# The start of a weight load and the order of all compute queues in an attention and GLU block on one core

## The chip, the cores and the metric

The kernel runs on one core of one Trainium2 chip. A core has a matrix engine (TensorE, here PE; its weight loads are shown apart as PEld), a vector engine (VectorE, DVE), a scalar engine (ScalarE, ACT), a general engine (GpSimd, POOL) and SyncE (SP), which here only issues DMA transfers. Each engine works through its own queue in order, and engines wait for one another by semaphores. Matrix products land in PSUM, which has eight banks of 2 KB in each of 128 partitions; everything else lies in SBUF.

The metric is the device time of one execution in microseconds (us); lower is better. Results are given as a median over several executions, and one further execution is recorded by the hardware profiler.

## The reference

The reference is a transformer block of two halves on one sequence of S = 2048 tokens with D = 448 channels, in bfloat16. The first half is a linear attention with a learned feature map (16 heads of 28 channels), the second a gated feed-forward part with F = 1792.

```python
B, S, D = x.shape
H = 16; Dh = D // H
n = _layernorm(x)                                   # (x - mean) / sqrt(var + 1e-5)
q, k, v = split((n @ wqkv), heads)                  # each (H, S, Dh)
pq = einsum("bhsd,hdf->bhsf", q, w_phi)
pk = einsum("bhsd,hdf->bhsf", k, w_phi)
phi_q = concatenate([_softmax(pq), _softmax(-pq)], axis=-1)     # 56 features
phi_k = concatenate([_softmax(pk), _softmax(-pk)], axis=-1)
kv = einsum("bhsf,bhsd->bhfd", phi_k, v)            # sums over all 2048 tokens
z  = einsum("bhsf->bhf", phi_k)
num = einsum("bhqf,bhfd->bhqd", phi_q, kv)
den = einsum("bhqf,bhf->bhq", phi_q, z)[..., None] + 1e-6
h = x + (num / den) @ wo
n2 = _layernorm(h)
out = h + (_sigmoid(n2 @ w_gate) * (n2 @ w_up)) @ w_down
```

The sums `kv` and `z` need every token, so no token's `num` can be computed before the last token has been added to them. That is the one full stop in the middle of the block.

## The kernel before, in words

**Tiles.** The sequence is cut into 16 tiles of 128 tokens, numbered 0 to 15; `name_t` or `namet` is the operation `name` on tile `t`. Four tiles make a chunk of 512 tokens, numbered by `c`. The 448 channels are held as four slabs of 128 rows that overlap in part, and most matrix products run as two chains at once, one on rows 0 to 63 and one on rows 64 to 127 of the array. The helper `both` (L328, its matmul on L333) issues them alternately, so nearly all of PE's work stands under line 333 in the profile, and is told apart by its tensors. A product cut in two such steps has the names `...a` and `...b`.

**The graph and its order.** The function `build` describes 1029 operations with what each reads and writes. `Graph` derives the waits from that. The order on each engine is not derived: it is written out by hand in the dictionary `ORDER` (L249 on), one list of names for each of the queues `sp`, `act`, `pe`, `dve` and `pool`. An operation that may run on several engines runs on the one in whose list its name stands. The dictionary `PACE` (L312) adds further dependencies by hand: `{"ld_wg1": "kva14"}` lets the load `ld_wg1` wait until PE has finished `kva14`. Since queues are in order, whatever stands behind a waiting operation waits with it.

**The first stage: keys and values.** For each tile, DVE takes the statistics (`bst` L552, `agg` L553). POOL takes the power -1/2 of the variance (`pow1`, L561) and, where the normalising engine needs it, the negated mean (`nm1`, L560) and their product (`nb1`). `xn` (L580) normalises, on DVE, POOL or ACT, into one of five buffers. Tiles 0 to 3 are transposed on PE (`xT0` to `xT3`) and copied out by `xT0e` to `xT3e` (L538); tiles 4 to 15 are transposed by DMA on SP's queue (`xT`, L590). Meanwhile the feature map is folded into the key and the query weights: `w2m0` (keys, from a PE transpose `wT`) and `w2m1` (queries, from DMA transposes `ld_q0` to `ld_q3`, L507), both L619, with the copies `w2e0` (L628) and `w2e1` (L636). `warm` operations are products of zeros.

Then PE makes a tile's key features in bank 0 or 1 and its values in bank 2 or 3: `ppa ppb vva vvb` for two tiles at once (tiles 0 to 3), `pva pvb` for one (tiles 4 to 15). ACT takes the exponentials of the features and of the negated features (`ek`, two instructions, L678 and L679), DVE or ACT copies the values (`v1`, L538). DVE sums (`ss`, L682) and inverts (`rs`, L688), and POOL or DVE multiplies (`phi`, L692). There are five buffers for `ek` and `v1` and four for `phi`. `kva` and `kvb` add a tile's products into banks 6 and 7 (L333, `psum<-v,phi`). `seed` writes there first.

**Queries and output of the attention.** `pqa` and `pqb` make the query features of a chunk in two banks, `eqc_ip` and `eqc_im` (ACT, L730) their exponentials. After the last `kv` step, `kvzA` to `kvzD` copy the sums with a mask out of banks 6 and 7 (DVE L759 or ACT L763). `qs` sums the exponentials of tiles 0 and 1. For each tile follow `num` on PE, and `rsm qq b c rden` on DVE (L807 to L815), which put the two softmaxes' shares together; `o` divides (L819, POOL or DVE) and `oT` transposes (PE for tiles 0 and 1, else DMA). `wof` or `woa` and `wob` multiply with `wo`; `h` adds the residual (L845), and `nm sq ve pow2 hn hT` (L849 to L868) are the second layer norm and its transpose (DVE or POOL, ACT, DVE or POOL, POOL, DVE or POOL, SP).

**The gated part.** The chunks of it are named by their first tile and cover 2, 2, 4, 4 and 4 tiles: 0, 2, 4, 8 and 12. For each of 14 slices `f` of F, `gac_f` and `gbc_f` make gate and up products in two banks, `sig` (ACT, L919) takes the sigmoid into one of four buffers, and `hh` (L925) multiplies. For the names in `UCOPY` (most of chunk 0 and all of chunk 2) ACT first copies the up product into one of the five `xn` buffers (`uc`, L924), and then `hh` may run on POOL as well as on DVE. `dn dp dm dl` multiply with `w_down`; `fin` (L959) adds the residual and `out` stores.

**Loads.** SP's queue issues the loads in this order: tiles of `x`, the key, value and query weights, the transposes `xT4` to `xT15`, `wo` (784 KB in four transfers), gate and up weights (`ld_wg0 ld_wu0` to `ld_wg3 ld_wu3`, 448 KB each, two of them half of that), `w_down` (224 KB each), then the transposes and stores of the rest. All load instructions stand on L434. PE asks for all eight gate and up loads at once, in the empty operation `wgu`, ahead of `num6` and `ga0_1`.

**What the change touches.** `ORDER` and `PACE`, and through `ORDER` the engine on which 33 operations run. The functions that follow take their order and their engine from these two.

Of the kernel before, what the change touches and what calls it, by code (L numbers as in the profile page):

```python
# [18 lines left out]
class Graph:  # L19
# [109 lines left out]
    def emit(self, nc):  # L129
# [120 lines left out]
    ),  # L250
    "act": (
# [11 lines left out]
    ),  # L263
# [22 lines left out]
    ),  # L286
    "dve": (
# [15 lines left out]
    ),  # L303
    "pool": (
# [5 lines left out]
    ),  # L310
}
PACE = {"ld_wg1": "kva14"}  # L312
UCOPY = "0_2 0_3 0_4 0_5 0_6 0_7 0_8 0_9 0_10 0_11 0_12 0_13 2_0 2_1 2_2 2_3 2_4 2_5 2_6 2_7 2_8 2_9 2_10 2_11 2_12 2_13".split()
PROGRAM = (
# [35 lines left out]
def build(nc, A_x, A_wqkv, A_w_phi, A_wo, B_w_gate, B_w_up, B_w_down, out):  # L350
# [10 lines left out]
    with ExitStack() as es:  # L361
# [630 lines left out]
        at = {o.name: o.i for o in g.ops}  # L992
        for a, b in PACE.items():
            g.ops[at[a]].deps[at[b]] = False
# [36 lines left out]
```

## Time and profile before

| | |
|---|---|
| Median of 3 executions | 205.1 us (204.98 to 205.74) |
| The profiled execution | 205.9 us |
| Its span, first to last instruction | 204.0 us |
| Granted PE clock | 1.00 |
| PE busy | 195.4 us (96%) |
| PE weight loads | 112.7 us (55%) |
| DVE busy | 127.1 us (62%) |
| ACT busy | 99.8 us (49%) |
| POOL busy | 67.1 us (33%) |
| DMA | 16.25 MB, mean 80 GB/s |

Times inside the execution are counted from the start of the span. A row of the groups or of a timeline gives the line of the program, the engine, the instruction and its tensors (result, arrow, inputs), partitions and elements, and how many there are. In a timeline the first number is the start and the second the time; a square bracket at the end says how long the engine had stood idle just before, and which engine and tile ended that. "issue" there means that the engine waited for nothing that the profile shows. A row of the busy time by stage gives the stretch and its length, then busy time and instructions of PE, PEld, DVE, ACT and POOL, the granted clock, the share of time in which a DMA engine was busy, and GB/s. In the rows of the DMA queues, q1 carries the loads and stores, q8 and q14 instructions.

### The profile page before, as it was taken

The page shows a single profiled execution, that of the slowest core. Times are in us where ns is not written, and L with a number is a line of the kernel's source. Part 1 is how long each engine was busy: PE and PEld are TensorE (multiplying, and loading weights), DVE is VectorE, ACT ScalarE, POOL GpSimd, SP SyncE. Part 2 cuts the span into 40 slices and gives each one's busy share as a digit, 9 for nine tenths or more (in the row PEclk, how much of TensorE's full clock was granted, in tenths as well). Part 3 has the DMA queues.
Part 4 walks back from the last instruction along what each step waited for, and adds up shares of the span by engine and source line. Part 5 has one row for each costly group of instructions (what it writes and reads, how often), then busy time and mean ns, then how long its engine had stood idle before and what let it go on. Part 6 is the DMA issues. An engine that isn't in the chain of part 4 may idle for free.

```text
span 204.0 us, 5889 instructions
## 1 busy us (share of the span) xinstructions
PE 195.4 (96%) x2500; PEld 112.7 (55%) x2500; DVE 127.1 (62%) x310; ACT 99.8 (49%) x217; POOL 67.1 (33%) x106
## 2 busy tenths in 40 slices
PE   7879999989979999989999999999999999999995
PEld 2835565656548876667444544555555555454443
DVE  6896999968999862336668967526532422262224
ACT  3766988987796767345332343323522222222220
POOL 5497969930634857932024020001400000000000
PEclk9999999999999999999999999999999999999999
DMA  6965445828995231121007501030212000004002
GB/s 148 318 142 124 54 74 86 249 93 246 297 191 143 55 72 39 26 55 26 5 0 80 122 19 36 3 76 23 51 37 67 0 0 5 0 3 135 0 0 90
DMA packets 32867, 16.25 MB, mean 80 GB/s; under 512 B 25097, under 2 KB 31945, under 8 KB 32841
## 3 DMA queue, kind: packets, MB, share of 16 engines
q1 hardware_dynamic: 32336, 15.86, 34.0%
q8 instruction: 19, 0.31, 0.6%
q10 hardware_dynamic: 504, 0.03, 0.2%
q14 instruction: 8, 0.06, 0.1%
HBM read 8.34 MB, written 1.84 MB: 50 GB/s over the span
## 4 chain that ended last, share of the span: by engine, by line
PE 89%; SPq 5%; DMA 2%; issue 1%; DVE 1%; ACT 0%
PE psum L333 82%; PE psum L952 5%; SPq L434 3%; DMA WqT<-in_A_wqkv_dram 2%; SPq L507 2%; PE psum L894 1%; PE psum L619 1%; PE psum L545 0%; DVE b_sb L810 0%; DVE c_sb L813 0%; PE psum L892 0%; ACT sg_sb L919 0%; DVE xnT L538 0%; PE psum L716 0%; DVE x_sb L959 0%
## 5 line engine op out<-in xcount | busy, mean ns | idle before, releaser
L333 PE MATMUL psum<-xnT,wg_sb 64*128 64x512 bf16 (+1 forms) x490 | 93.5, 333 | 0.8 <-ACT xn_pad L924 0.7
L333 PE MATMUL psum<-xnT,wu_sb 64*128 64x512 bf16 (+1 forms) x490 | 93.3, 333 | 0.0
L919 ACT ACTIVATE sg_sb<-psum 128x512 bf16<-128x512 f32 (+1 forms) x70 | 35.7, 516 | 80.4 <-PE psum L333 79.9
L925 DVE TENSOR_TENSOR hhT<-sg_sb,psum 128x512 bf16<-128x512 bf16 (+1 forms) x44 | 28.9, 671 | 46.8 <-ACT sg_sb L919 46.5
L333 PEld LDWEIGHTS psum<-xnT,wg_sb 64*128 64x128 bf16 x490 | 44.4, 94 | 22.6 <-DVE hhT L925 2.2
L333 PEld LDWEIGHTS psum<-xnT,wu_sb 64*128 64x128 bf16 x490 | 44.4, 94 | 13.3
L333 PE MATMUL psum<-wd_sb,hhT 64*128 64x448 bf16 x336 | 37.2, 349 | 0.0
L333 PEld LDWEIGHTS psum<-wd_sb,hhT 64*128 64x128 bf16 x336 | 17.4, 94 | 14.4 <-DVE x_sb L845 0.5
L333 PE MATMUL psum<-wv_sb,xnT 64*128 64x448 bf16 x112 | 22.3, 351 | 0.0
L333 PE MATMUL psum<-Wk,xnT 64*128 64x448 bf16 x112 | 22.1, 350 | 0.0
L854 POOL TENSOR_SCALAR ve<-ssq 128x1 f32<-128x1 f32 x14 | 3.1, 222 | 47.0 <-ACT junk L851 46.4
L692 POOL TENSOR_TENSOR phi<-hhT,rs 128x896 bf16<-128x896 bf16 x10 | 17.1, 1727 | 1.4 <-PE psum L333 1.4
L682 DVE TENSOR_REDUCE ss<-hhT 128x32 f32<-128x896 bf16 x16 | 16.8, 1063 | 0.0
L730 ACT ACTIVATE eq<-psum 120x1024 bf16<-120x1024 f32 x16 | 15.7, 1026 | 0.9 <-PE psum L333 0.8
L819 POOL TENSOR_TENSOR o_pad<-c_sb,rden 128x448 bf16<-128x448 bf16 x11 | 10.2, 935 | 17.2 <-DVE rden L815 17.1
L333 PE MATMUL psum<-xnT,Wq 64*120 64x512 bf16 x112 | 15.0, 384 | 0.2
L845 DVE SCALAR_TENSOR_TENSOR x_sb<-psum,x_sb 128x448 bf16<-128x448 f32 x14 | 8.3, 620 | 5.9 <-PE psum L333 5.8
L959 DVE SCALAR_TENSOR_TENSOR x_sb<-psum,x_sb 128x448 bf16<-128x448 f32 (+2 forms) x17 | 9.4, 592 | 4.2 <-PE psum L333 2.3
L333 PE MATMUL psum<-wo_o,oT 64*128 64x448 bf16 x49 | 11.5, 349 | 0.0
L333 PE MATMUL psum<-wo_e,oT 64*128 64x448 bf16 x49 | 11.5, 349 | 0.0
L952 PE MATMUL psum<-wd_sb,hhT 128*128 128x448 bf16 (+2 forms) x70 | 11.2, 316 | 0.0
L924 ACT CAST xn_pad<-psum 128x256 bf16<-128x256 f32 x26 | 9.5, 379 | 3.0 <-PE psum L333 3.0
(111 smaller groups left out, 255.3 us busy)
## 6 DMA issues: line engine op xcount, KB each, us to landing
out_dram<-x_sb SPq DMA_DIRECT2D x15, 112.0 KB, 1.8
x_sb<-in_A_x_dram SPq DMA_DIRECT2D x7, 224.0 KB, 4.5
wd_sb<-in_B_w_down_dram SPq DMA_DIRECT2D x7, 224.0 KB, 4.4
wg_sb<-in_B_w_gate_dram SPq DMA_DIRECT2D x3, 448.0 KB
wu_sb<-in_B_w_up_dram SPq DMA_DIRECT2D x3, 448.0 KB
wv_sb<-in_A_wqkv_dram SPq DMA_DIRECT2D x2, 224.0 KB, 4.8
wk_sb<-in_A_wqkv_dram SPq DMA_DIRECT2D x2, 196.0 KB, 3.8
wo_e<-in_A_wo_dram SPq DMA_DIRECT2D x1, 336.0 KB, 3.2
```

Of the source, the lines that this page charges most:

```text
L333: p = e.matmul(o, lhsT=w, rhs=r, start=st, stop=sp, tile_position=(row, 0))
L434: return op(eng, name, lambda e: e.dma_start(dst, src), r=r, w=w, dma="in" if eng == "sp" else "ain", nring=(48 if eng == "sp" else 8) if ...
L682: op("dve", "ss%d" % t, lambda e: e.tensor_reduce(ss[:, s, :].rearrange("p (b h) -> p b h", h=2), eks.rearrange("p b (d h) -> p b h d", h= ...
L692: return e.tensor_tensor(phi[:, sp, :, :, :].rearrange("p b a n -> p (b a) n")[:, :, 0:56].rearrange("p b (d h) -> p b d h", h=2), eks.rea ...
L730: op("act", "eq%d_%d%s" % (c, i, "pm"[sg]), lambda e, sg=sg: e.activation(eq[c][:, sg, 2 * i:2 * i + 2, :].rearrange("p g n -> p (g n)"), ...
L819: return e.tensor_tensor(o_pad[:, t % NO, off:off + D].rearrange("p (h d) -> p h d", h=H), c_sb[:, t % NS, :, 0:DH], rden[:, t % NS, :][:, ...
L845: op("dve", "h%d" % t, lambda e: e.scalar_tensor_tensor(out=h_sb[:, t, :], in0=bk(b)[:, 0:D], scalar=1.0, in1=x_sb[:, t, :], op0=ALU.mult, ...
L919: op("act", "sig" + nm, lambda e: e.activation(sg_sb[:, k, 0:N], bk(bg)[:, 0:N], ACT.Sigmoid), r=[B(bg)], w=[("sg", k)])
L924: op("act", "uc" + nm, lambda e: e.copy(up, bk(bu)[:, 0:N]), r=[B(bu)], w=[ub])
L925: op(("pool", "dve") if nm in UCOPY else "dve", "hh" + nm, lambda e: e.tensor_tensor(hhT[(t0 // 4) % NHH][:, ff, ns], sg_sb[:, k, 0:N], up ...
L952: p = e.matmul(bk(b)[:, lo:hi], lhsT=hb[:, ff, TS(t)], rhs=wd_sb[:, ff, lo:hi], start=ff == 0, stop=ff == FT - 1)
L959: op("dve", "fin%d%s" % (t, nm), lambda e: e.scalar_tensor_tensor(out=h_sb[:, t, lo:hi], in0=bk(b)[:, lo:hi], scalar=1.0, in1=h_sb[:, t, l ...
```

## The change

`PACE` gets a second entry: `ld_wg0`, the first of the gate and up loads, now waits until PE has finished `pvb15`, the last projection of the first stage. In SP's list, which is unchanged, `ld_wu0` and then all further loads stand behind it.

The lists of the four compute engines are written anew. PE's, ACT's and POOL's differ from the old ones up to the middle of chunk 2 of the gated part, DVE's up to `fin1` in the same stretch; behind that all lists are as before. Besides the order, these operations change engine:

- from ACT to POOL: `nm1_2`, `nm1_3`, `nm1_12`; from ACT to DVE: `v1_13`, `w2e1_0`, `xT2e`, `kvzA`;
- from DVE to ACT: `v1_2`, `v1_10`, `kvzB`;
- from DVE to POOL: `phi1`, `phi4`, `o6`, `nm2`, `nm3`, `nm7`, `hh0_3`, `hh0_8`, `hh0_11`;
- from POOL to DVE: `phi3`, `phi8`, `o8`, `ve2`, `ve4`, `ve6`, `ve7`, `hn4`, `hn5`, `hn6`, `hh0_2`, `hh0_5`, `hh0_7`, `hh2_1`.

```diff
     "act": (
-        "wphi3 wphi2 wphi1 wphi0 kvzones wTe0 wTe1 xT1e wTe3 w2e0_0 w2e0_2 nm1_2 w2e0_3 nm1_3 xT2e ek0 ek1 v1_1 v1_0 "
-        "w2e1_0 w2e1_1 ek2 ek3 v1_3 nm1_8 w2e1_3 v1_4 ek4 w2e1_2 ek5 v1_5 xn10 ek6 v1_6 ek7 v1_7 ek8 v1_8 ek9 nm1_12 "
-        "v1_9 eq0_0m ek10 ek11 v1_11 ek12 v1_12 ek13 v1_13 eq0_0p ek14 ek15 v1_14 v1_15 eq0_1m par eq0_1p eq1_0p kvzA "
...
+        "wphi3 wphi2 wphi1 wphi0 kvzones wTe0 wTe1 xT1e wTe3 w2e0_0 w2e0_2 w2e0_3 ek0 ek1 v1_0 v1_1 ek2 w2e1_1 nm1_8 "
+        "v1_2 ek3 v1_3 w2e1_3 v1_4 ek4 w2e1_2 ek5 v1_5 xn10 ek6 v1_6 ek7 v1_7 v1_8 ek8 eq0_0m ek9 v1_9 ek10 v1_10 "
+        "ek11 v1_11 ek12 v1_12 ek13 eq0_0p par ek14 ek15 v1_14 v1_15 eq0_1m eq0_1p eq1_0m kvzB eq1_0p eq1_1p eq1_1m "
...
     "pe": (
...
-        "warm9 ppa0 xT2 ppb0 vva0 xT3 vvb0 w2m1_1 w2m1_0 ppa2 vva2 ppb2 vvb2 w2m1_2 seed w2m1_3 pva4 kvb0 pvb4 kva1 "
-        "pva5 kva0 pvb5 pva6 pqa0_0 pvb6 pva7 kvb1 kva2 pvb7 kvb2 pva8 kvb3 kvb5 pvb8 pva9 kva3 kvb4 kva5 pvb9 kva4 "
-        "pva10 pqb0_0 pvb10 pva11 kva6 pvb11 kvb6 pva12 kvb7 pvb12 pva13 kva7 kvb8 pvb13 kva8 pva14 kva9 pvb14 pva15 "
-        "kvb9 kva10 pvb15 pqa0_1 kvb12 kvb10 pqb0_1 kvb11 kva12 pqa1_0 kva11 kva13 pqb1_0 kvb13 kva14 kvb15 kva15 "
-        "kvb14 pqa1_1 qs pqb1_1 wwo num0 num1 pqa2_0 pqb2_0 num2 pqa2_1 pqb2_1 oT0 num3 oT1 wof0 wof1 num4 pqa3_0 "
...
-        "ga0_10 gb0_11 gb0_10 wob6 num10 ga0_13 ga0_12 gb0_13 gb0_12 dn0_0 dn0_4 ga2_0 ga2_1 gb2_0 gb2_1 dn0_8 dn0_11 "
-        "ga2_2 ga2_3 gb2_2 dp0_0 gb2_3 ga2_4 dp0_4 ga2_5 gb2_4 dp0_8 gb2_5 dp0_11 ga2_6 ga2_7 gb2_6 gb2_7 woa8 ga2_8 "
+        "ppa0 warm9 ppb0 vva0 xT2 xT3 vvb0 ppa2 ppb2 vva2 w2m1_1 vvb2 seed w2m1_0 w2m1_3 kva0 pva4 kvb0 pvb4 pva5 "
+        "w2m1_2 kva1 pvb5 pva6 pqa0_0 pvb6 kvb1 pva7 kvb2 kva3 pvb7 pva8 kvb3 kva2 pvb8 pqb0_0 pva9 kvb4 pvb9 pva10 "
+        "kva4 kvb5 pvb10 kva5 pva11 kvb6 pvb11 pva12 kva6 kvb7 pvb12 kva7 kvb8 pva13 kva8 pvb13 pva14 kvb10 pvb14 "
+        "pva15 kva10 kvb9 pvb15 kva9 pqa0_1 kvb12 kva11 pqb0_1 pqa1_0 kvb13 kvb11 kva12 pqb1_0 kvb14 kva13 kva15 "
+        "kvb15 kva14 qs pqa1_1 wwo num0 pqb1_1 num1 pqa2_0 num2 pqb2_0 pqa2_1 oT0 pqb2_1 num3 oT1 wof0 wof1 num4 "
...
+        "ga0_10 gb0_11 gb0_10 wob6 num10 ga0_13 ga0_12 gb0_13 gb0_12 dn0_0 dn0_4 ga2_1 ga2_0 gb2_1 gb2_0 dn0_8 dn0_11 "
+        "ga2_2 ga2_3 gb2_2 gb2_3 dp0_0 ga2_4 dp0_4 ga2_5 gb2_4 gb2_5 dp0_8 dp0_11 ga2_6 ga2_7 gb2_6 gb2_7 woa8 ga2_8 "
...
     "dve": (
...
-        "bst5 agg4 bst11 agg5 bst7 bst8 bst10 agg7 bst6 bst9 agg6 xT3e ss0 agg10 agg8 rs0 ss1 agg11 bst12 rs1 v1_2 "
-        "agg9 phi1 agg12 ss2 ss3 rs2 bst13 ss4 bst14 rs3 bst15 ss5 agg14 agg15 rs5 rs4 agg13 phi5 ss6 phi4 xn12 rs6 "
-        "xn13 ss7 ss8 rs7 xn14 v1_10 rs8 ss9 ss10 rs9 ss11 rs10 rs11 phi11 ss12 rs12 ss13 rs13 ss14 ss15 rs14 rs15 "
-        "phi14 phi15 kvzB kvzC kvzD rsm0 qq0 b0 b1 c0 c1 rden0 rsm2 rden1 qq2 b2 c2 oT0e rsm3 qq3 rden2 b3 c3 bs2_0 "
...
-        "hh0_0 rsm7 qq7 b7 c7 rden7 hh0_3 h2 h3 rden6 o6 rsm8 qq8 b8 c8 rden8 h4 rsm9 nm2 h5 qq9 hh0_6 b9 nm3 c9 nm4 "
-        "h7 hh0_9 h6 hh0_8 rsm10 rden9 hh0_13 hh0_10 qq10 nm5 hh0_11 nm7 hh2_2 b10 c10 fin1 fin0 rden10 hh2_5 hh2_4 "
+        "bst5 bst7 agg4 agg5 bst6 agg7 agg6 bst11 bst8 bst10 xT2e xT3e agg8 agg11 ss0 bst9 rs0 agg10 bst12 agg9 ss1 "
+        "ss2 rs1 bst13 w2e1_0 agg13 ss3 rs2 bst14 bst15 agg12 rs3 ss4 agg15 agg14 phi3 ss5 ss6 rs4 xn12 rs6 rs5 ss7 "
+        "phi5 ss8 rs7 rs8 xn13 xn14 ss9 ss10 rs10 phi8 ss11 rs9 rs11 ss12 v1_13 rs12 phi11 ss13 rs13 ss14 ss15 rs14 "
+        "rs15 phi14 phi15 kvzC kvzD kvzA rsm0 qq0 b0 c0 b1 rden0 rsm2 c1 qq2 rden1 b2 c2 oT0e rden2 rsm3 qq3 b3 c3 "
...
+        "hh0_1 hh0_0 rsm7 qq7 b7 c7 rden7 h3 rden6 h2 rsm8 qq8 b8 hh0_2 c8 rden8 o8 ve2 hh0_5 h4 h5 rsm9 qq9 hh0_7 b9 "
+        "hh0_6 nm5 c9 h6 h7 ve4 rsm10 rden9 hh0_9 hh0_10 hh0_13 ve6 qq10 ve7 b10 c10 hh2_2 nm4 hn6 hn4 hh2_1 hn5 fin1 "
...
     "pool": (
-        "epsl0 v1ones neghalf epsr0 ident0 ident pow1_1 phipad opad0 pow1_0 pow1_2 pow1_3 xn2 wqpad xn3 nm1_4 pow1_4 "
-        "xn4 xn5 pow1_6 nm1_6 xn6 phi0 xn7 pow1_8 xn8 xn9 nb1_8 phi2 xn11 phi3 pow1_12 phi6 xn15 phi7 phi8 phi9 phi10 "
-        "phi12 phi13 o0 o1 o2 o3 pow2_1 pow2_0 o5 o4 o7 ve2 hh0_2 pow2_2 hh0_4 hh0_5 o8 hh0_7 hn2 ve3 pow2_3 hn3 nm6 "
-        "o9 ve6 ve4 hh0_12 pow2_6 ve5 hn6 hh2_0 pow2_4 hn4 ve7 pow2_7 pow2_5 hn5 hh2_3 hh2_1 hh2_6 hh2_7 hh2_8 hh2_9 "
...
+        "epsl0 v1ones neghalf epsr0 ident0 ident pow1_1 phipad opad0 pow1_0 pow1_2 pow1_3 nm1_2 wqpad nm1_3 xn2 xn3 "
+        "nm1_4 pow1_4 pow1_6 nm1_6 xn4 xn7 xn5 xn6 phi0 pow1_8 phi1 xn8 xn9 nb1_8 phi2 xn11 pow1_12 phi4 phi6 nm1_12 "
+        "phi7 xn15 phi10 phi9 phi12 phi13 o0 o1 o2 o3 pow2_0 pow2_1 o5 o4 o7 nm3 o6 hh0_3 hh0_4 ve3 nm2 pow2_2 hn2 "
+        "pow2_3 hn3 hh0_8 hh0_11 nm6 ve5 hh0_12 pow2_4 o9 hh2_0 pow2_6 pow2_7 nm7 hh2_3 pow2_5 hh2_6 hh2_7 hh2_8 "
...
-PACE = {"ld_wg1": "kva14"}
+PACE = {"ld_wg0": "pvb15", "ld_wg1": "kva14"}
```

39 rows, old and new, of the table ORDER are left out of this document.

## The prediction

> **What bounds the kernel now.** I read the page's first part, the PE's waits, the busy time by stage, and then the timelines around each PE gap.
>
> ```profile
> PE 195.4 (96%) x2500; PEld 112.7 (55%) x2500; DVE 127.1 (62%) x310; ACT 99.8 (49%) x217; POOL 67.1 (33%) x106
> PE psum L619 <- DMA WqT<-in_A_wqkv_dram: 1.4, 1, 1.4
> PE psum L333 <- DVE c_sb L813: 1.0, 1, 1.0
> PE psum L333 <- issue: 0.9, 1, 0.9
> PE psum L333 <- ACT xn_pad L924: 0.7, 1, 0.7
> 18.50:44.00 25.50, 25.50 (x438) 15.46 (x439) 25.25 (x47) 23.57 (x52) 21.07 (x16) 1.00 0.54 117
> 47.30:60.80 13.50, 12.35 (x192) 6.81 (x189) 12.40 (x36) 10.89 (x14) 4.76 (x6) 1.00 1.07 260
> 61.00:86.60 25.60, 25.60 (x453) 20.05 (x447) 16.04 (x54) 16.61 (x51) 17.90 (x31) 1.00 0.32 69
> 88.00:184.00 96.00, 95.90 (x1050) 50.69 (x1052) 49.91 (x115) 31.66 (x69) 10.33 (x22) 1.00 0.16 31
> ```
>
> The stage rows give the length, then busy time and instructions of PE, PEld, DVE, ACT, POOL, the clock, the DMA share and GB/s. PE is busy 96%, but for two different reasons. From 61 on its queue is simply full: 95.90 of 96.00, with the other engines half idle. What happens there is worth only what it adds to or takes from PE's gaps. From 18.5 to 44 PE is also recorded as busy, but DVE works 25.25 of 25.50 and ACT 23.57: PE's products wait for banks that ACT empties, and ACT and PE for phi. DVE sets this stage. From 47.3 to 60.8 DVE is again nearly full (12.40 of 13.50). So a gain comes from three places: an earlier start or less work for DVE before 44, the four PE gaps, and nothing else. The gaps together are 4.0 us.
>
> **The start: `w2m1_1` goes behind `ppa2 ppb2 vva2`.**
>
> ```profile
> 13.33 0.56 ACT L679 ACTIVATE hhT<-psum 128x448 bf16<-128x448 f32 x1
> 13.29 0.38 DVE L538 COPY xnT<-psum 128x512 bf16<-128x512 bf16 x1
> 15.19 0.55 PE L619 MATMUL psum<-Wphi,WqT 112*128 112x112 bf16 x8 [1.43 <-DMA WqT<-in_A_wqkv_dram]
> 17.97 0.54 ACT L678 ACTIVATE hhT<-psum 128x448 bf16<-128x448 f32 x1 [1.10 <-PE psum L333]
> 18.54 0.63 DVE L538 CAST v<-psum 128x448 bf16<-128x448 f32 x1 [1.69 <-PE psum L333]
> 15.78 1.09 ACT L636 CAST Wq<-psum 128x224 bf16<-128x224 f32 x4 [1.00 <-PE psum L619]
> 11.21 0.24 POOL L560 TENSOR_SCALAR nm<-mv 128x2 f32<-128x2 f32 x1
> 13.04 2.53 SPq L590 DMA_TRANSPOSE xnT<-xn_pad  x2
> 19.34 0.36 PE L333 MATMUL psum<-Wk,xnT 64*128 64x448 bf16 x1
> ```
>
> PE stands 1.43 for the transposed Wq while `ppa2`, queued behind it, has its inputs: `ek1` ended at 13.33 + 0.56 = 13.89, `xT3e` at 13.29 + 0.38 = 13.67. In the new order `ppa2` can start near 14.0 in place of 15.7. `ek2`, which started at 17.97, follows `ppb2` and comes about 1.6 earlier, and `ss2` with it. DVE then meets no hole: the 1.69 it sat idle before `v1_2` goes. `vva2` covers what is left of the Wq wait.
>
> DVE's own work changes. In: `xT2e` 0.38, `w2e1_0` (half of ACT's 1.09, so 0.55, taken as 0.6), `v1_13` 0.63, `phi3` and `phi8`. Out: `v1_2` and `v1_10` (0.63 each), `phi1` and `phi4`. The phi cancel; net 0.38 + 0.6 + 0.63 - 1.26 = +0.35. ACT gives up three `nm1`, `xT2e`, `w2e1_0` and one `v1` and takes two: about 1.3 less, hidden, since DVE is the bound. POOL takes three `nm1` (0.24 each) and runs both rstd steps ahead of `xn4` and `xn7` ahead of `xn5`. So `xT4` to `xT6`, and what follows them on SP, leave later by about 0.8; but `xT4`, issued at 13.04, was first used at 19.34, and after the change PE still comes to it near 18, so I cost that at nothing (0.8 without that cover). `pqb0_0` and its exponential `eq0_0m` go ahead of `pva9` and `ek9`: the same work on PE and ACT. `phi10` goes ahead of `phi9` on POOL, and `ek14` waits for `phi9`'s buffer; `eq0_0p` fills that wait on ACT.
>
> **The port.** The same move has a price.
>
> ```profile
> L692 POOL TENSOR_TENSOR phi<-hhT,rs x10: 1679/1688/2066, 15.5 to 40.7; 128x896 bf16<-128x896 bf16 x10
> L692 DVE TENSOR_TENSOR phi<-hhT,rs x6: 574/608/800, 19.2 to 43.4; 128x896 bf16<-128x896 bf16 x6
> 36.74 0.80 DVE L692 TENSOR_TENSOR phi<-hhT,rs 128x896 bf16<-128x896 bf16 x1
> 31.57 0.67 DVE L580 TENSOR_SCALAR xn_pad<-x_sb,mv,rst 128x512 bf16<-128x512 bf16 x1
> L925 DVE TENSOR_TENSOR hhT<-sg_sb,xn_pad x14: 227/286/670, 65.8 to 97.9; 128x256 bf16<-128x256 bf16 x14
> 82.99 0.67 DVE L925 TENSOR_TENSOR hhT<-sg_sb,xn_pad 128x256 bf16<-128x256 bf16 x1 [4.15 <-ACT xn_pad L924]
> 82.75 0.77 POOL L860 TENSOR_SCALAR hn_pad<-x_sb,nm,rst 128x512 bf16<-128x512 bf16 x1
> ```
>
> Durations by line are min/median/max in ns. Some DVE instructions stretch when POOL is at work: `hh2_2` took 0.67 against a median of 0.286, and ended (83.66) just after POOL's `hn4` (83.52). `phi11` took 0.80 against 0.608, and the longest POOL phi (2.066 against 1.688) is the one beside it; `xn14` took 0.67 against an `xn` of 0.3 to 0.4. So before, collisions cost DVE 0.2 + 0.35 = 0.55 in this stage, mostly because five of six DVE phi fell where POOL had no long instruction. After, `phi3`, `phi5`, `phi8` and `phi11` and the three `xn` all fall where POOL works without pause. Bounds: nothing more than before, or a whole POOL phi each. Laying the new queues beside each other with these durations, POOL ends `phi1` near 20.6 and, after `xn8`, `xn9` and `nb1_8`, runs `phi2` from 22.2 to 23.9; DVE reaches `phi3` at 23.4 and waits 0.4 to 0.5. Further on POOL's `phi4`, `phi6` and `phi9` end just where DVE's `phi5`, `xn13` and `phi11` come, 0.1 to 0.2 each. That is 0.95 in all, so +0.4.
>
> [...]
>
> So phi15, the last, ends earlier by 1.69 - 0.35 - 0.4 = **0.94** (bounds: 1.7 earlier to 2.5 later).
>
> **The gate and up loads.**
>
> ```profile
> 36.09 1.12 SPq L434 DMA_DIRECT2D wo_o<-in_A_wo_dram  x2
> 37.25 0.59 SPq L434 DMA_DIRECT2D wg_sb<-in_B_w_gate_dram  x1
> 45.51 0.47 SPq L434 DMA_DIRECT2D wg_sb<-in_B_w_gate_dram  x1
> 41.00:42.00 1.00, 1.00 (x28) 0.68 (x26) 0.99 (x2) 1.00 (x3) 1.00 (x1) 1.00 0.87 337
> 42.00:43.00 1.00, 1.00 (x26) 0.70 (x24) 1.00 (x4) 1.00 (x2) 0.41 (x1) 1.00 0.27 93
> 43.00:44.00 1.00, 1.00 (x28) 0.64 (x23) 1.00 (x2) 1.00 (x3) 0.00 (x0) 1.00 0.00 0
> 45.06 1.01 PE L333 MATMUL psum<-v,phi 64*128 64x58 bf16 x37 [0.86 <-issue]
> 40.37 0.54 ACT L678 ACTIVATE hhT<-psum 128x448 bf16<-128x448 f32 x1
> 42.86 1.16 DVE L692 TENSOR_TENSOR phi<-hhT,rs 128x896 bf16<-128x896 bf16 x2
> 46.12 1.23 DVE L759 TENSOR_TENSOR kvz<-psum,mask 64x232 bf16<-64x232 f32 x3 [2.10 <-PE psum L333]
> q8 instruction: 19, 0.31, 0.6%
> ```
>
> At 45.06 PE had stood 0.86 in the middle of one `kv` operation, for nothing that the profile shows, with phi15 ready since 44.02. Queue q8 brings instructions, 19 packets of 0.31 / 19 = 16 KB. My reading: one of them was due while wo, `ld_wg0` and `ld_wu0` (784 + 896 KB) held the DMA engines, got through only when these drained near 42.5, and was late. With the new wait, `ld_wg0` leaves when `pvb15` ends (`ek15` starts on it, 40.37 in this trace, and about 39.4 after), the wo loads (784 KB, under 3 us at the 337 GB/s of the first row) drain first, and the packet passes. So **-0.86**. Against it: the DMA was empty for 1.2 us before PE stopped. Bounds: -0.86 to +0.86 (another packet late, behind the moved loads).
>
> What is queued behind the new wait on SP: `ld_wu0`, then `ld_wg1`, which waits for `kva14` anyway, and the rest after it. 896 KB move from 37.3–42.5 to about 41–44, before the later loads start; the last gate/up load follows `kva14` as now, and earlier with it. Cost 0; if the DMA engines failed to keep up, `ga0_1` would wait for what is late.
>
> From phi15's end (44.02) to `kvz` (46.12) were 2.10; 0.86 is that gap. In the new order three `kv` steps follow phi15 (37 matmuls, 8 a step, took 1.01 here, so some 0.2 each), which makes about 0.7 in place of 1.24. But `kvb13` and `kvb11` now stand ahead of `pqb1_0` and hang on POOL's phi13. I take **-0.2** (bounds 0 to -0.5).
>
> **From `kvz` to the gate.** One masked copy changes place between ACT and DVE, `qs` goes ahead of `pqa1_1`, `b` and `c` interleave otherwise. DVE has 1.1 idle in 13.5 and the same instructions; the wait for `c5` (1.0 in PE's waits) stays, shifted. Cost 0 (bounds -0.4 to +0.3).
>
> **The gate stage.**
>
> ```profile
> 85.83 1.29 POOL L925 TENSOR_TENSOR hhT<-sg_sb,xn_pad 128x256 bf16<-128x256 bf16 x2
> 87.22 0.38 ACT L919 ACTIVATE sg_sb<-psum 128x256 bf16<-128x256 f32 x1 [1.16 <-PE psum L333]
> 87.92 0.28 PE L333 MATMUL psum<-xnT,wg_sb 64*128 64x256 bf16 x1 [0.72 <-ACT xn_pad L924]
> ```
>
> POOL finished `hh2_1` at 87.12, behind `hn4`, `hn5` and `hh2_3`. `sig2_5` needs its buffer (87.22; PE had long been done), `ga2_7` needs `sig2_5` and `uc2_5`, and PE stood 0.72. The change gives `hh2_1` to DVE, ahead of `hn5`, and issues `gb2_5` earlier: **-0.8**, the gap and a little of the drained pipeline. Bounds: -0.88 to 0. `ve6` now stands on DVE ahead of `qq10`, `b10` and `hh2_2` and waits for `sq6`, which ACT now does only after `uc2_1`; DVE was idle 4.15 there already, so it is covered. `hn4` to `hn6` go to DVE and `hT6` leaves a little later; the first product that reads it, `ga4_1`, waits for `hT7`, much later, anyway. The other exchanged hh (`hh0_2`, `hh0_5`, `hh0_7` to DVE; `hh0_3`, `hh0_8`, `hh0_11`, `o6` to POOL) cost 0.29 each on DVE and 0.65 on POOL and fit in the idle of the row 61 to 86.6 (DVE 9.5, POOL 7.7). Uncovered, a late hh costs PE what it is late. From `ga2_10` all is as before and PE is full, so every gain reaches the end.
>
> **Sum.** -0.94 - 0.86 - 0.2 - 0.8 = -2.8. The profiled execution took 205.9 (span 204.0); it would take 203.1. The median shown is 205.1, so I predict **202.3**.
>
> **The rivals.**
> - *The port eats the start's gain (slower).* If the seven DVE instructions find POOL in the middle of a phi, each waits about 0.8, 5.4 in all or 4.85 more than before. phi15 is then 1.69 - 0.35 - 4.85 = 3.5 late and the sum +1.65: 206.8. It turns the sign above 0.54 a piece. For it: POOL is busy 21.07 of 25.5. Against: POOL's phi start when DVE has finished `rs`, so the two go in step. Chance 0.20.
> - *The 0.86 gap stays, or another comes, so the wait does not do what it may.* For it: the empty DMA before the stop. 202.3 + 0.86 + 0.2 = 203.4. Chance 0.14. [...]
> - *POOL or ACT sets the first stage instead*, POOL's `xn` and phi being later behind the moved `nm1` and rstd: 0.94 is lost, 203.2. Chance 0.15.
> - *Both of the last two:* 204.4. Chance 0.08.
> - *A hole in the gate stage* (hh, `ve6` or `hn` late for PE): 1 to 2.5 given back, 203.3 to 204.8. Chance 0.07.
>
> **The numbers.** The forecast has 0.36, and a range of its own of 201.2 to 203.3. What a measurement of this kernel can tell from no change is 0.5%, 1.0 us. Faster by more than that (under 204.1): 0.36 + 0.14 + 0.15 + 0.03 = 0.68. Same: 0.08 + 0.04 + 0.02 = 0.14. Slower: 0.18. The range 201.0 to 206.0 leaves out most of the first rival above, and the case that all bounds fall well below.
>
> **What would show it.** Right: no PE wait for WqT, or a short one; no DVE idle near 17 to 18.5; no issue gap near 44; DVE's `kvz` at about 44.1; the first `ga` 2.0 earlier than now; no PE wait for ACT near 85; PE otherwise full. Wrong: DVE phi well over 0.6 and phi15 after 44 (the first rival); an issue gap of PE at another place (the second); DVE idle between 20 and 42 (the third); a new PE wait for ACT or DVE between 60 and 90 (the last).

## The result and the profile after

The changed kernel takes 203.53 us (median of 11, 202.60 to 204.43) against 204.81 (median of 11, 203.66 to 205.74) for the kernel before: a ratio of 0.9938, 95% interval 0.9914 to 0.9962, or 1.3 us less. The forecast was 202.3, with a range of its own of 201.2 to 203.3; the range given with the chances was 201.0 to 206.0. The profiled execution took 203.83, with a span of 202.0 against 204.0. In the rows below the changed kernel's line numbers are one higher than before (its text is a line longer); in the experiments some are one lower.

The changed kernel's waits of PE (total us, times, longest), and its busy time by stage, with the columns of the prediction's stage rows:

```profile
PE psum L532 <- DVE zero L439: 1.2, 1, 1.2
PE psum L607 <- DMA wk_sb<-in_A_wqkv_dram: 1.0, 1, 1.0
PE psum L334 <- DVE c_sb L814: 1.0, 1, 1.0
PE psum L334 <- DVE phi L693: 0.7, 1, 0.7
```

```profile
18.50:44.20 25.70, 25.05 (x433) 14.79 (x434) 25.41 (x48) 22.83 (x48) 21.09 (x17) 1.00 0.56 126
45.20:59.60 14.40, 13.41 (x219) 7.76 (x212) 13.48 (x38) 12.24 (x17) 4.83 (x6) 1.00 1.05 236
60.00:85.00 25.00, 25.00 (x447) 20.96 (x440) 18.09 (x59) 16.59 (x52) 15.31 (x26) 1.00 0.43 76
86.00:182.00 96.00, 95.90 (x1054) 51.32 (x1050) 50.85 (x117) 31.61 (x69) 10.34 (x22) 1.00 0.16 32
```

Three of the four PE waits that the prediction named are gone: for WqT, the issue gap, and the one for ACT near 88. One is new, 0.7 for a DVE phi. From 60 on PE is full (25.00 of 25.00 and 95.90 of 96.00), as before. But DVE's first stage, 25.41 of 25.70, is no shorter than it was. The timeline of DVE and POOL shows what stood in it, and the end of the stage:

```profile
30.63 2.01 DVE L581 TENSOR_SCALAR xn_pad<-x_sb,mv,rst 128x512 bf16<-128x512 bf16 x2
30.75 1.74 POOL L693 TENSOR_TENSOR phi<-hhT,rs 128x896 bf16<-128x896 bf16 x1
...
43.06 1.16 DVE L693 TENSOR_TENSOR phi<-hhT,rs 128x896 bf16<-128x896 bf16 x2
45.19 1.24 DVE L760 TENSOR_TENSOR kvz<-psum,mask 64x232 bf16<-64x232 f32 x3 [0.97 <-PE psum L334]
```

phi15 ends at 43.06 + 1.16 = 44.22, where it ended at 44.02 before. The two xn of the first row, xn13 and xn14, took 2.01 us; xn13 alone is 0.31 of it, xn14 1.78 (they overlap by 0.08). xn14 came 0.11 us after POOL's phi7 had begun (30.75) and ended just after it (32.64 against 32.49).

To compare executions I cut the span at events that both kernels have, each read from the timelines: the start of ppa0, the end of phi15, the start of the first `kvz`, the end of c5, the start of ga2_7, and the end of the last `fin`. The further traces of each kernel come from the experiments.

| us | ppa0 starts | ppa0 to phi15 | phi15 to kvz | kvz to c5 | c5 to ga2_7 | ga2_7 to end |
|---|---|---|---|---|---|---|
| before, profile shown | 10.07 | 33.95 | 2.10 | 14.49 | 27.31 | 114.05 |
| before, 2nd trace | 10.56 | 33.93 | 0.99 | 14.49 | 27.31 | 114.05 |
| before, 3rd trace | 9.84 | 33.34 | 1.01 | 14.49 | 27.31 | 114.05 |
| after, profile shown | 10.50 | 33.72 | 0.97 | 14.38 | 26.40 | 114.05 |
| after, 2nd trace | 9.77 | 33.73 | 0.97 | 14.39 | 26.40 | 114.05 |

The sections from `kvz` on repeat to 0.01 us. So the gate stage is worth 0.91 and the stage ahead of it 0.10, in every execution. What differs between executions is the start (the last transposed query weights, whose issue no list moves, land at 14.21 to 15.53 in the three traces of before), the first stage, and the issue gap, which was there in one of three traces of the kernel before. The mean of ppa0 to phi15 is 33.74 before and 33.73 after. Three more traces with the old first stage come from the experiments (the wait alone, one product of the gate stage, no wait on any load): 33.86, 33.10 and 33.16, so the mean of six is 33.56. Two more with the changed first stage have 32.89 and 34.00, and the mean of four is 33.59. Either way the first stage won nothing that these traces can tell. One thing the table hides: in the new order the products of zeros `warm9` run behind ppa0 and not ahead of it, which starts ppa0 itself 0.11 earlier after `w2m0`.

### The profile page after: what moved, and what is told of

It is laid out like the page before. It is cut to its first block, busy times and chain, and to the rows that moved or that the text cites. A ratio compares the mean times of both kernels' runs of the same rounds, so it can differ in the third digit from the quotient of the medians.

```text
span 202.0 us, 5879 instructions
## 1 busy us (share of the span) xinstructions
PE 195.5 (97%) x2500; PEld 114.7 (57%) x2500; DVE 130.6 (65%) x317; ACT 99.0 (49%) x212; POOL 65.0 (32%) x104
## 3 DMA queue, kind: packets, MB, share of 16 engines
HBM read 8.34 MB, written 1.84 MB: 50 GB/s over the span
## 4 chain that ended last, share of the span: by engine, by line
PE 90%; DVE 4%; DMA 2%; SPq 1%; ACT 1%; issue 1%
PE psum L334 81%; PE psum L953 5%; DMA wk_sb<-in_A_wqkv_dram 2%; DVE ss L683 2%; DVE xn_pad L581 1%; PE psum L620 1%; PE psum L532 1%; SPq L435 1%; PE psum L895 1%; PE psum L546 1%; DVE rs L689 0%; DVE b_sb L811 0%; PE psum L607 0%; DVE c_sb L814 0%; ACT v L539 0%
## 5 line engine op out<-in xcount | busy, mean ns | idle before, releaser
L920 ACT ACTIVATE sg_sb<-psum 128x512 bf16<-128x512 f32 (+1 forms) x70 | 35.2, 514 | 75.3 <-PE psum L334 74.8
L334 PEld LDWEIGHTS psum<-wd_sb,hhT 64*128 64x128 bf16 x336 | 17.9, 94 | 14.0 <-DVE x_sb L846 0.5
L693 POOL TENSOR_TENSOR phi<-hhT,rs 128x896 bf16<-128x896 bf16 x10 | 17.7, 1775 | 2.8 <-DVE rs L689 2.6
L855 POOL TENSOR_SCALAR ve<-ssq 128x1 f32<-128x1 f32 x10 | 2.0, 202 | 45.6 <-ACT junk L852 45.3
L679 ACT ACTIVATE hhT<-psum 128x448 bf16<-128x448 f32 x16 | 8.8, 547 | 5.4 <-PE psum L334 5.2
```

The costliest lines, as they stand in the source:

```text
L334: p = e.matmul(o, lhsT=w, rhs=r, start=st, stop=sp, tile_position=(row, 0))
L679: e.activation(ek[:, s, :, 0, :], src, ACT.Exp)
L693: return e.tensor_tensor(phi[:, sp, :, :, :].rearrange("p b a n -> p (b a) n")[:, :, 0:56].rearrange("p b (d h) -> p b d h", h=2), eks.rea ...
L920: op("act", "sig" + nm, lambda e: e.activation(sg_sb[:, k, 0:N], bk(bg)[:, 0:N], ACT.Sigmoid), r=[B(bg)], w=[("sg", k)])
```

## The experiments

The unchanged kernel ran beside each group and had medians of 204.57, 204.33 and 204.46. All ratios are to it.

**The new wait alone.** The lists as before.

```diff
-PACE = {"ld_wg1": "kva14"}
+PACE = {"ld_wg0": "pvb15", "ld_wg1": "kva14"}
```

> The kernel before with the new wait alone (the load of the first gate weights waits for pvb15; all lists as before). Theory 1, the loads hold up an instruction packet of PE: the issue gap of 0.86 us at 45.06 goes, nothing else changes, so 0.7 to 0.9 us less than before (about 204.0). Theory 2, the gap has nothing to do with the loads: it stays, same time as before. If the later loads are late for the gate stage, PE waits for a DMA near 61 and the time is longer than before.

204.63 us, ratio 1.0000 (0.9979 to 1.0021). Its trace has no issue gap, `kvz` starts 0.99 after phi15, and no PE wait for a DMA is new. So the time that theory 1 promised did not come. That the wait took the gap out isn't shown by this one trace either: two traces of the unedited kernel (below) have none.

**The change without the new wait.**

```diff
-PACE = {"ld_wg0": "pvb15", "ld_wg1": "kva14"}
+PACE = {"ld_wg1": "kva14"}
```

> The changed kernel without the new wait (all lists as changed). Theory 1: an issue gap of PE of 0.5 to 0.9 us is back between 43 and 47, and the time is that much above the changed kernel's 203.5 (204.0 to 204.4). Theory 2: no gap comes back, 203.5.

203.34 us, ratio 0.9931 (0.9905 to 0.9956): the changed kernel's time within the intervals, and no gap in the trace. With these lists the wait does nothing that these runs can tell.

**The kernel before, twice more.** These two had no edit.

> The kernel before, unchanged, once more. If PE's issue gap near 45 belongs to the program, it is there again with 0.8 to 0.9 us; if it depends on how the instruction packet and the loads fall in one execution, it may be absent or elsewhere, and then the run with the wait alone could not win it in its median.

> The kernel before, unchanged, a third time: is PE's issue gap near 45 there? It was in the first trace (0.86) and in that with hh2_1 moved (0.9), and absent in the second trace of the same kernel. Also phi15 should end 28.96 us after the last transposed query weights land, as in all traces with the old lists.

PE's `kv` products and DVE's `kvz`, first in the run with `hh2_1` moved (below), which has the old lists and loads here, then in the second trace of the kernel before:

```profile
43.39 0.22 PE L332 MATMUL psum<-v,phi 64*128 64x58 bf16 x3
44.46 1.01 PE L332 MATMUL psum<-v,phi 64*128 64x58 bf16 x37 [0.85 <-issue]
45.52 1.23 DVE L758 TENSOR_TENSOR kvz<-psum,mask 64x232 bf16<-64x232 f32 x3 [2.10 <-PE psum L332]
```

```profile
44.47 0.97 PE L333 MATMUL psum<-v,phi 64*128 64x58 bf16 x40
45.48 1.23 DVE L759 TENSOR_TENSOR kvz<-psum,mask 64x232 bf16<-64x232 f32 x3 [0.99 <-PE psum L333]
```

The gap was there in two of four traces with the old lists and loads (the first, and that with `hh2_1` moved), and absent in the second and third of the kernel before. Where it was, PE had the same 1217 instructions of the trace behind it, and the packet on q8 had begun at 42.74 and 41.99; where it wasn't, at 39.46 and 40.78. phi15 ended 28.96 or 28.97 us after the last transposed query weights landed in all four, as expected. That landing came 4.98, 4.97 and 4.37 after ppa0 began in the three traces of the kernel before: this is the difference between 33.95 and 33.34 in the table.

The traces also show when such a packet is too late. PE works some 6.8 us on the 256 instructions ahead of the place of the gap, and in every trace the packet for what follows began after PE had started on them. Where PE stopped, it went on 2.32 and 2.47 after the packet began. By these figures the packet has some 4.3 us to begin in (an estimate: 6.8 less 2.5). In the two traces with the gap it began 5.50 and 5.35 after PE started on the 256; in the two without, 1.74 and 4.39, the latter just in time; with the wait alone, 1.46; with only the query weights later, 4.29; in all seven with the changed first stage, 0.7 to 3.2, with the new wait or without.

**No wait on any gate or up load.** The kernel before with more of the suspected cause.

```diff
-PACE = {"ld_wg1": "kva14"}
+PACE = {}
```

> The kernel before with no wait on any gate or up load: all eight leave from 37.3 on, 2.7 MB in place of 0.9 MB, so the suspected cause of PE's issue gap is tripled. Theory 1, the instruction packet stands behind the loads: at the 337 GB/s seen there the loads keep the DMA engines busy until about 45.5, the packet comes then, and PE's issue gap grows from 0.9 to 3 to 4 us; the time is 2 us or more above before. Theory 2, the loads don't matter for it: the gap stays at 0.9 or is absent, same time as before.

208.13 us, ratio 1.0192 (1.0145 to 1.0239), 3.8 us longer by the medians and 3.9 by the ratio. PE's timeline of this run, and the row of its waits:

```profile
44.15 1.01 PE L332 MATMUL psum<-v,phi 64*128 64x58 bf16 x37 [0.30 <-issue]
51.79 0.59 PE L332 MATMUL psum<-xnT,Wq 64*120 64x512 bf16 x3 [2.61 <-issue]
```

```profile
PE psum L332 <- issue: 2.9, 2, 2.6
```

Theory 1 holds, one packet further: PE stops for 0.30 after 1217 instructions and for 2.61 after 1473, which is 256 more, about what one packet of q8 brings (an estimate: the page of before has 5000 matmuls and weight loads and 19 packets, 263 each if all are PE's). The packet for the second began at 49.20, 5.06 after PE started on the 256 instructions ahead of it, and PE went on 2.59 later. The first stop, the one that the theory named, did not grow; its packet began 4.68 after PE started on the 256 instructions ahead of that one. The DMA engines were full until about 51 (share 1.05 from 50 to 51, 0.69 in the next us) and not 45.5, so the next packet met the loads too. The section from phi15 to `kvz` is 0.56 longer than without a gap and that from `kvz` to c5 2.94, so nearly all of the time lies around these two stops. So in this run the loads held up PE's instructions, for 0.30 and 2.61.

**One product of the gate stage.** The kernel before with one operation moved.

```diff
-"dve":  ... hh0_11 nm7 hh2_2 b10 c10 ...
+"dve":  ... hh0_11 nm7 hh2_1 hh2_2 b10 c10 ...
-"pool": ... hn5 hh2_3 hh2_1 hh2_6 ...
+"pool": ... hn5 hh2_3 hh2_6 ...
```

> The kernel before with one product moved: hh2_1 from POOL to DVE, ahead of hh2_2. If POOL's late hh2_1 is the whole cause of PE's wait of 0.72 us before ga2_7, that wait goes and the time is 0.7 to 0.9 us below before (about 204.0). If another wait stands right behind it (the next sigmoid or copy late as well), less than 0.3 us is won.

203.53 us, ratio 0.9961 (0.9934 to 0.9988): 0.8 us less. In its trace c5 to ga2_7 is 26.43, 0.88 below before, and PE's wait for ACT is gone. One operation is the whole gain of this stage but 0.03.

**The first stage alone.** All five lists as changed up to the last `kv` step, phi15 and `eq0_1p`; behind that, and the loads, as before.

> The kernel before with the new lists for the first stage alone (up to the last kv step, phi15 and eq0_1p); the rest of the lists and the loads as before. What the moved product (0.8) and the wait (0 by the run with the wait alone) leave of the change's 1.28 us is about 0.5. Theory: the first stage is worth that, 0.3 to 0.7 us below before. Rival, the first stage gains the full 1.1 us that was predicted for it and the interplay with the rest loses some: 1.0 or more below before.

204.35 us, ratio 0.9999 (0.9983 to 1.0016): nothing. The same two rows as in the changed kernel:

```profile
29.73 2.01 DVE L580 TENSOR_SCALAR xn_pad<-x_sb,mv,rst 128x512 bf16<-128x512 bf16 x2
29.77 1.82 POOL L692 TENSOR_TENSOR phi<-hhT,rs 128x896 bf16<-128x896 bf16 x1
```

xn14 stood here too, and phi15 ended 34.00 after ppa0 began.

**Only the query weights later.** The kernel before, no engine changed.

```diff
-"pe":  ... vvb0 w2m1_1 w2m1_0 ppa2 vva2 ppb2 vvb2 w2m1_2 seed w2m1_3 pva4 kvb0 pvb4 kva1 pva5 kva0 ...
+"pe":  ... vvb0 ppa2 ppb2 vva2 w2m1_1 vvb2 w2m1_0 seed w2m1_3 pva4 kvb0 pvb4 kva1 pva5 w2m1_2 kva0 ...
-"act": ... v1_0 w2e1_0 w2e1_1 ek2 ek3 v1_3 nm1_8 ...
+"act": ... v1_0 ek2 w2e1_1 ek3 v1_3 w2e1_0 nm1_8 ...
```

> The kernel before with one move alone: w2m1 (the products that wait for the transposed query weights) behind ppa2, ppb2 and vva2 on PE, and its copies w2e1_0 and w2e1_1 behind ek2 on ACT; no operation changes engine. Theory: DVE's idle time before v1_2 goes (1.69 us in the profile of before) and with no added DVE work the time falls by 0.8 to 1.5 us. Rival, something else is late in the first stage (phi on POOL, xn and the transposes, or ACT, which must now do w2e1_0 later): 0.3 us or less is won.

204.18 us, ratio 0.9992 (0.9971 to 1.0013): at most 0.6 is won. DVE's row for `v1_2`:

```profile
17.90 0.63 DVE L537 CAST v<-psum 128x448 bf16<-128x448 f32 x1 [0.69 <-PE psum L332]
```

PE no longer waits for WqT, and still DVE idles 0.69 here and 0.47 later, before `v1_10`, both times for PE, which itself had stood 0.28 for ACT at 14.39: in this trace ACT and PE come next as limits. phi15 ends 33.15 after ppa0 begins. Here WqT landed 4.74 after ppa0 began, for which the old lists would give 28.96 + 4.74 = 33.70, so 0.55 is won in this trace.

**The three xn together.** The changed kernel with DVE's list edited.

```diff
-... ss6 rs4 xn12 rs6 rs5 ss7 phi5 ss8 rs7 rs8 xn13 xn14 ss9 ...
+... ss6 xn12 xn13 xn14 rs4 rs6 rs5 ss7 phi5 ss8 rs7 rs8 ss9 ...
```

> The changed kernel with DVE's xn12, xn13 and xn14 put together ahead of rs4, where POOL waits for rs4 and has nothing to run. Collision theory: xn14, which took 1.78 us beside POOL's phi7 in the changed kernel against 0.31 for xn13, takes about 0.31, phi15 ends 1.0 to 1.5 us earlier, and the time is 1.0 to 1.5 us below the changed kernel's 203.5 (202.0 to 202.5). Rival, PE, ACT or POOL sets the stage as soon as DVE has air: DVE stands idle somewhere between 27 and 42 instead, and 0.3 us or less is won.

203.12 us, ratio 0.9921 (0.9893 to 0.9949). The expected 1.0 did not come. DVE's timeline:

```profile
28.85 0.96 DVE L691 TENSOR_TENSOR phi<-hhT,rs 128x896 bf16<-128x896 bf16 x1
32.85 1.09 DVE L681 TENSOR_REDUCE ss<-hhT 128x32 f32<-128x896 bf16 x1 [0.48 <-ACT hhT L678]
```

xn14 took 0.40, but POOL's phi4, released by rs4, was 1.0 later (counted from ppa0), phi5 ran into it (0.96 against 0.56), and DVE then stood 0.48 for `ek10`. phi15: 33.42.

**xn13 and xn14 ahead of rs7.** The changed kernel with DVE's list edited, and then the smaller edit, one swap.

```diff
-... ss8 rs7 rs8 xn13 xn14 ss9 ...
+... ss8 xn13 xn14 rs7 rs8 ss9 ...
```

> The changed kernel with DVE's xn13 and xn14 ahead of rs7 and rs8. In the changed kernel's trace xn14 starts 0.11 us after POOL's phi7, which rs7 releases, and stands 1.47 us; here phi7 can't start before xn14 is done. Theory, the first stage's gain is eaten by this one collision: xn14 takes about 0.4 us, xn13 at most 0.3 more (beside the end of phi6), phi15 ends 32.6 to 33.1 us after ppa0 begins in place of 33.7, and the time is 0.5 to 1.0 us below the changed kernel's. Rival: PE, ACT and DVE are so even in this stage that another wait takes its place, as with the three xn ahead of rs4; then phi15 stays at 33.4 or later and at most 0.3 us is won.

```diff
-... ss8 rs7 rs8 xn13 xn14 ss9 ...
+... ss8 rs7 xn13 xn14 rs8 ss9 ...
```

> The changed kernel with one swap: rs8 behind xn14 on DVE. xn14 then comes 0.3 us earlier, so about 0.2 us before phi7 in place of 0.11 us behind it. If who comes first decides, xn14 takes 0.3 to 0.4 us and phi7 waits a little, phi15 ends about 32.9 us after ppa0 begins, and the time is 0.5 to 1.0 us below the changed kernel's. If it is a matter of overlap alone, xn14 or phi7 is stretched by a similar amount and nothing is won.

202.31 us, ratio 0.9896 (0.9878 to 0.9913), and 202.36 us, ratio 0.9899 (0.9878 to 0.9919). Both beat both kernels; against the changed one it is 0.4% by these ratios, 0.8 us, of which the intervals (0.9878 to 0.9913 and 0.9914 to 0.9962) leave little doubt for the first and some for the second. phi15 ends 33.07 and 32.90 after ppa0 begins. The rows of the one swap, DVE and POOL:

```profile
29.77 0.64 DVE L579 TENSOR_SCALAR xn_pad<-x_sb,mv,rst 128x512 bf16<-128x512 bf16 x2
30.14 1.82 POOL L691 TENSOR_TENSOR phi<-hhT,rs 128x896 bf16<-128x896 bf16 x1
```

The two xn take 0.64 in place of 2.01, and phi7 1.82 in place of 1.74 (1.82 too in the run of the first stage alone, where xn14 came behind it). In the changed kernel xn14 began 0.11 after phi7 and lost 1.47; here it begins 0.13 ahead of phi7, and phi7 is 0.08 longer.

**The change once more**, no edit.

> The changed kernel, unchanged, once more. If the collision of xn14 with phi7 belongs to the program, it is there again with 1.78 us; in the trace of the changed lists without the new wait it was absent (0.41), with the same order, so it may depend on a few tenths of a us in one execution.

```profile
29.91 2.01 DVE L581 TENSOR_SCALAR xn_pad<-x_sb,mv,rst 128x512 bf16<-128x512 bf16 x2
30.03 1.74 POOL L693 TENSOR_TENSOR phi<-hhT,rs 128x896 bf16<-128x896 bf16 x1
```

The collision is there again to the hundredth. Of the four traces with the changed first stage it is in three; in that without the new wait xn14 came 0.13 ahead of phi7, took 0.41, and phi15 ended 32.89 after ppa0 began.

## Why the prediction was right and wrong

The sign was right, and 203.53 lies in the range of 201.0 to 206.0, but not in the forecast's own of 201.2 to 203.3. Of the four terms of the sum one came, the gate stage, and the sign rests mostly on it. That the second rival's 203.4 was nearly met is chance: that rival keeps the 0.94 of the first stage, which did not come. The sum of -2.8 against the measured -1.3 breaks down by its steps.

- **Gate stage, -0.8: right.** -0.91 in the traces, -0.8 in the median of the run with `hh2_1` alone. POOL's late `hh2_1` was the cause, and nothing was late behind it.
- **The gate and up loads, -0.86: wrong.** That loads hold up a packet of PE's instructions was right for the run with all loads free, where PE stopped for 0.30 and 2.61. The step that failed is taking a gap seen in one profiled execution as part of every one. It was in two of four traces, and the wait alone was worth nothing in its median (a gain up to 0.4 isn't excluded). In that one execution it cost more than was put down: phi15 to `kvz` is 2.10 with it and 0.99 to 1.01 without.
- **phi15 to `kvz`, -0.2: wrong.** 0.97 to 1.01 in all traces without the gap, before and after. What I took for slack to be won, 1.24, was a part of the gap.
- **`kvz` to the gate, 0:** -0.10.
- **The first stage, -0.94: wrong.** DVE's idle time went as forecast; it has no wait over 0.12 from 13.4 to phi15. The stage no longer hangs on WqT: that landed 4.83 and 3.80 after ppa0 began in the two traces of the changed kernel, and ppa0 to phi15 is 33.72 and 33.73. The added work was 0.67 (`w2e1_0`) + 0.42 (`xT2e`) + 0.61 (`v1_13`) - 1.26 = +0.44, near the +0.35 put down. The term that was mis-sized is the one headed the port, the collisions of DVE with POOL: +0.4 was taken, and beside the unhindered 0.31 and 0.56 of the same trace xn14 lost 1.47, phi3 0.25 and phi5 0.12, together 1.84 against 0.55 before: +1.3. Besides, 1.69 is the largest idle time of six traces with the old first stage, which have 0.84 to 1.69 as WqT lands early or late, 1.28 in the mean. The run with the one swap shows the size: without xn14's wait ppa0 to phi15 is 32.90, 1.05 below the execution that the forecast was worked from and 0.66 below the mean of the six, where -0.94 was forecast. The run without the new wait shows the same with the changed order itself: there xn14 came first, and the stage took 32.89.
- **The port as a rival:** the collisions that it counted on are what decided, and phi15 after 44, the sign named for it, came (44.22); its form did not. I had let seven instructions wait 0.8 each (5.6 in all, where the text has 5.4), which no run shows: one waited 1.47, and of the rest phi3 lost 0.25 and phi5 0.12. In the text I had put phi3's wait at 0.4 to 0.5 and no wait at all on xn14. What the two engines share, no run shows; the traces show that the order counts: 0.11 behind phi7, xn14 took 1.78, and 0.13 ahead of it, with the one swap, both xn together took 0.64 and phi7 was 0.08 longer. My layout of the queues by hand, good to some tenths, could not tell these apart.
- **The base.** The profiled execution of before held the gap and a late WqT. The forecast took all its idle time as belonging to the kernel, and then took the gain off the lower median. Later medians of the kernel before were 204.3 to 204.8. (The rival with both losses adds up to 204.3, where the text has 204.4.)

The parts add up: -0.91 - 0.10, -0.11 for the earlier ppa0, and 0 for the first stage make -1.1 in traces without the gap. The remaining 0.2 of the median's 1.3 lies inside its interval, and a gap of 1.1 in a part of the executions of before would also give it; the runs don't tell these two apart. Why the packet begins late in one execution and not in the next also stays open.

## What to carry to other kernels

Before a stall is counted as a gain, look whether a second execution of the same kernel has it: stalls on transfers and on instruction packets came and went here (PE's wait for WqT was 1.43, 1.41 and 0.81 in the three traces of the kernel before, its issue gap 0.86 in the first and absent in the others), while from `kvz` on the waits between engines repeated to a hundredth. The collision of DVE and POOL, which here hung on 0.24 us (0.11 behind or 0.13 ahead), was in three of four traces. In the first stage, where DVE and POOL were busy 25.41 and 21.09 of 25.70, the order around the release of a long POOL instruction mattered more than the number of instructions moved: with xn13 and xn14 ahead of rs7, which releases phi7, the ratio was 0.9896 in place of 0.9938. And in that stage, with PE, DVE and ACT busy 25.50, 25.25 and 23.57 of 25.50 before, a wait that was taken out came back smaller (DVE's 1.69 before `v1_2` as 0.69), so undo a suspected collision on the chip before building on its price.

## What the runs showed of the hardware

That one DVE instruction began 0.24 us earlier against POOL's (0.13 ahead in place of 0.11 behind) took away a loss of 1.47 us on DVE and left POOL's instruction 0.08 longer. Loads of 2.7 MB sent at once stopped PE for 2.61 us with no wait that the profile could name, 256 instructions after a first stop of 0.30, so here a PE stop of kind "issue" was a transfer's doing; PE went on 2.32 to 2.59 us after the packet began in all four stops. And with equal lists everything from `kvz` on repeated to 0.01 us (three traces of before, two of the changed kernel); the spread between executions of one kernel lay ahead of it, in when the first transfers landed (14.21 to 15.53 for WqT) and in such a packet (phi15 to `kvz` 2.10 with the gap, 0.99 and 1.01 without).
